# The output product of a gated MoE chunk in seven products of eight on token halves, for 12 of 24 chunks

## Chip, cores and metric

The kernel runs on one core of one Trainium2 chip. The metric is the device time of one execution in microseconds (us); lower is better. Three executions of the kernel before took 2841.73 to 2842.45 us, median 2842.4 us.

## What is computed

The reference takes a real tensor of 4 x 3072 x 256, transforms it by a Fourier transform along both axes, and passes the real part through two gated layers. The change lies at the end of the first layer:

```python
h = np.maximum(x @ w_in, 0.0)
u, v = (h[..., :d_ff // 2], h[..., d_ff // 2:])       # d_ff // 2 = 512
v_n = (v - mu) / np.sqrt(var + 1e-06)
v_s = np.einsum('ts,bsd->btd', w_spatial, v_n) + b_spatial[None, :, None]
gated = u * v_s
return (gated @ w_out).astype(np.float32)              # w_out: 512 x 256
```

The product `gated @ w_out` is what the kernel calls the second product: for each of 4 batches and 3072 tokens, 512 inner values and 256 outputs.

## The kernel before

All products run on TensorE in the type fp32r, each number being split in a high and a low part; a product is three matmuls (`mm3`, lines 259 to 263): high by high, high by low, low by high. ScalarE makes the high part (a cast), VectorE the low part (a subtraction).

**Stages.** Up to about 254 us the Fourier transform and the first layer's input product run, and U and V go to DRAM. From there to about 1752 us the spatial product `w_spatial @ v_n` runs, as two passes (p = 0, 1) over a pair of batches, each in seven block products instead of eight (`ORDER` = 3, 5, 1, 7, 4, 2, 6) of three token chunks of 512 columns (c = 0, 1, 2): 42 "leaves". After that the second layer runs to the end.

**A leaf** has six steps (`kp`). In each step TensorE does 24 matmuls of 512 columns: two k by four blocks d of 128 gate rows by three of `mm3`, into four PSUM banks. The banks of one leaf are `base` to `base + 3`, and the next leaf has the other four. While a leaf runs, VectorE works off the four banks of the leaf before (`evacuate`, step 0 to 3, one bank each). In the four products 5, 4, 2, 6 (`FINAL`) this yields the finished gate of a chunk: one operation makes `g` from the bank and the sums kept, mostly another one keeps a sum for later, line 1240 multiplies by `max(U, 0)`, ScalarE casts the high part (1246), VectorE makes the low part (1248). So there are 24 chunks with a second product, each done in the leaf behind its own.

**The second product before** (`second`, line 1276): at the end of step 4 for the output half o = 0, at the end of step 5 for o = 1. Each is four blocks d by `mm3` = 12 matmuls of 512 columns, into a bank that is already worked off; ScalarE copies the result (1287), and its queue sends both halves to DRAM (1289).

**Order on the queues.** Each engine works in order. In each step VectorE has first the `evacuate` of the leaf before, then the operands of three steps ahead (`advance`, `LEAD` = 3): where the block product needs it, a sum of two blocks of the spatial weights (933), and the low part (950); at the last chunk of a product also V blocks (929, 950). These take their ring slots as TensorE gives them back. SyncE's queue (SP) issues the loads in the order of the program; a load into a buffer in use waits there, and what is behind it waits too.

**U tiles** (`load_u`, 1257): four tiles of 128 x 512 for each chunk, in two buffers. U of d = 0 and 1 is loaded in step 4 of the chunk's own leaf; U of d + 2 is issued when line 1240 of d has been put into the program, and waits for that instruction.

**The last leaf** runs d by d from its third step on, its second product falls between the first groups of the second layer, and preparations for that layer (`split_wg`, `split_wv`, `x_steps`) run on VectorE and ScalarE meanwhile.

Of the kernel before, what the change touches and what calls it, by code (L numbers as in the profile page):

```python
# [10 lines left out]
F32 = mybir.dt.float32  # L11
# [12 lines left out]
DM = 256  # L24
# [136 lines left out]
def layouts(x, moe_w_in, moe_w_spatial, moe_b_spatial, moe_w_out, moe2_w_gate, moe2_w_val, moe2_w_out):  # L161
# [18 lines left out]
    for at in (0, 32, 64):  # L180
# [5 lines left out]
    wt = w.reshape(6, 512, 24, P).transpose(0, 3, 2, 1)  # L186
    wg, wv = (w.reshape(2, P, 12, P) for w in (moe2_w_gate, moe2_w_val))
    arrays = {
        "xh": xh,
# [4 lines left out]
        "bt": moe_b_spatial[tau].reshape(1, S),  # L194
        "w_out": moe_w_out.reshape(4, P, DM).transpose(1, 0, 2).reshape(P, 2, 512),

# [43 lines left out]
def tile_kernel(ctx: ExitStack, tc: tile.TileContext, t: dict, out: bass.AP):  # L240
# [926 lines left out]

    wo = [gp.tile([P, 2, 512], F32R, tag=f"wo{n}", name=f"wo{n}") for n in "hl"]
# [3 lines left out]
    taken, begun, stores = [], [], []  # L1172

    def background():

        new = lambda: gp.tile([P, 512], F32, tag="cv", name="cv", bufs=4)
        if taken:
            words, kind, i = taken.pop()
            begun.append((from64_first([words], new), kind, i))
        elif begun:  # L1180
            first, kind, i = begun.pop()
            value, = from64_rest(first, new())
            if kind == "second":
                split(wo[0][:, i, :], wo[1][:, i, :], value)
            elif kind == "out":
                stores.append((wv_d[i // 2][:, i % 2 * 512 : i % 2 * 512 + 512], value))
            else:

                a11, a12, a22, a21 = (value[:, k * P : k * P + P] for k in range(4))
                sums = new()  # L1190
                s1, s2, s3, s4 = (sums[:, k * P : k * P + P] for k in range(4))
                for s, x, y, op in (
                    (s1, a21, a22, ALU.add),
                    (s2, s1, a11, ALU.subtract),
                    (s3, a11, a21, ALU.subtract),
                    (s4, a12, s2, ALU.subtract),
                ):
                    nc.gpsimd.tensor_tensor(out=s, in0=x, in1=y, op=op)
                stores.append((wg_d[i][:, 0:384], value[:, 0:384]))
                stores.append((wg_d[i][:, 384:896], sums))  # L1200
        else:
            for to, value in stores:
                nc.sync.dma_start(to, value)
            stores.clear()
            if todo64:
                src, kind, i = todo64.pop(0)
                words = st_tile([P, 1024], U32, "words")
                load64(words, src)
                taken.append((words, kind, i))

    def evacuate(leaf, ps, d, side):
# [26 lines left out]
        if g is None:  # L1238
            return
        nc.vector.scalar_tensor_tensor(out=g, in0=side["u"][d], scalar=0.0, in1=g, op0=ALU.max, op1=ALU.mult)  # L1240
        if "parts" in side:
            gh, gl = (x[at] for x in side["parts"])
        else:
            gh = gp.tile([P, 512], F32R, tag="gh", name="gh", bufs=4)
            gl = gp.tile([P, 512], F32R, tag="gl", name="gl", bufs=4)
        nc.scalar.copy(gh, g)
        finish_gate(side)
        side["low"] = lambda: nc.vector.tensor_tensor(out=gl, in0=g, in1=f(gh), op=ALU.subtract)
        side["g"].append((gh, gl))
        if d < 2:  # L1250
            load_u(side, d + 2)

    def finish_gate(side):
        if "low" in side:
            side.pop("low")()

    def load_u(side, d):
        u = gp.tile([P, 512], F32, tag="u", name="u", bufs=2)
        nc.sync.dma_start(u, side["u_of"][:, d, :])
        side["u"].append(u)  # L1260

    def side_loads(leaf, side):
        p, i, c = leaf
        if i in (3, 4, 5):
            at = ((3 if i == 3 else 0) + c) * 512
            side["bias"] = gp.tile([P, 512], F32, tag="bias", name="bias")
            nc.sync.dma_start(side["bias"], t["bt"][:, at : at + 512].to_broadcast([P, 512]))
        if i in FINAL:
            mem, th = FINAL[i]
            at = (3 * th + c) * 512  # L1270
            side["u"] = []
            side["u_of"] = u_d[2 * p + mem][:, :, at : at + 512]
            for d in range(2):
                load_u(side, d)

    def second(leaf, o, bank, side):

        p, i, c = leaf
        mem, th = FINAL[i]
        finish_gate(side)  # L1280
        ps = banks(bank)
        for d in range(4):
            at = (d % 2) * 256 + o * P
            mm3(ps, [w[:, d // 2, at : at + P] for w in wo], side["g"][d], d == 0, d == 3)
        if o == 0:
            side["x2"] = gp.tile([P, 2, 512], F32, tag="x2", name="x2", bufs=1)
        nc.scalar.copy(side["x2"][:, o, :], ps)
        if o == 1:
            nc.scalar.dma_start(x2_d[(2 * p + mem) * 6 + 3 * th + c], side["x2"])

# [67 lines left out]
    def load_raw(j):  # L1358
        raw = []
        for c, n in zip(pairs[j], "hl"):  # L1360
            r = gp.tile([P, 2, 512], F32, tag=f"wo{n}", name="raw")
            nc.sync.dma_start(r, x2_d[c])
            raw += [r[:, 0, :], r[:, 1, :]]
        return raw
# [14 lines left out]
    for n, leaf in enumerate(leaves[:-1]):  # L1379
        p, i, c = leaf  # L1380
        base = 4 * (n % 2)
        ps = [banks(base + d) for d in range(4)]
        side = {"g": []}
        for kp in range(6):
            if before is not None:
                if kp < 4:
                    evacuate(before[0], before[1][kp], kp, before[2])
                else:
                    finish_gate(before[2])
            advance(6 * n + kp + LEAD, 2)  # L1390
# [4 lines left out]
            for k in range(2):  # L1395
                for d in range(4):
# [19 lines left out]
    ps = [banks(base + d) for d in range(4)]  # L1416
    side = {"g": []}
    raw = cp.tile([P, 4, 512], F32, tag="c12", name="raw0")
# [3 lines left out]
    for kp in range(2):  # L1422
# [8 lines left out]
        evacuate(before[0], before[1][kp], kp, before[2])  # L1431
    side_loads(leaf, side)
    advance(6 * n + 5, 0)
    finish_job()
    for d in (2, 3):
        evacuate(before[0], before[1][d], d, before[2])
    finish_gate(before[2])
    wv0 = [cp.tile([P, 8, DM], F32R, tag=f"c1{k}", name=f"wv{k}") for k in range(2)]
# [4 lines left out]
    for d in range(4):  # L1443
        for kp in range(2, 6):
            product(ps, leaf, kp, d)
        if d == 0:
            split_wg(0, staged_b[0])
            split_wv(0, staged_b[1])
        if d < 3:
            evacuate(leaf, ps[d], d, side)  # L1450
        if d == 1:
            second(before[0], 0, 4 - base + 2, before[2])
            split_wg(1, staged_b[2])
# [6 lines left out]
        if d == 2:  # L1460
            second(before[0], 1, 4 - base + 3, before[2])
            for step in steps[2:6]:
                step()
    before = (leaf, ps, side)
    wst = A["w"].tile([P, 1024], F32, tag="wl", name="wst")
# [34 lines left out]
    def gates(n):  # L1500
        g = G[n]
        nc.vector.tensor_tensor(out=g["s2"], in0=g["s2"], in1=g["t7"], op=ALU.mult)
        g["g"] = [[gp.tile([P, 512], F32R, tag="g" + x, name="g" + x, bufs=4) for x in "hl"] for _ in range(2)]

    def p67(n, prev):
        g = G.get(n)
        if g:
            g["t2"] = gp.tile([P, 512], F32, tag="cv", name="t2", bufs=4)
            g["t7"] = gp.tile([P, 512], F32, tag="u", name="t7", bufs=2)
            part(g["a"], n, "s2", "t2")  # L1510
            nc.scalar.copy(g["t2"], g["a"])  # L1511
# [15 lines left out]
    def outputs(n, k, os=(0, 1)):  # L1527
# [6 lines left out]
        if fb == 11:  # L1534
            c = pairs[j][k]
            at = slice(c * 512, c * 512 + 512)
            last = j + 1 == len(pairs)
            ot = gp.tile([P, 2, 512], F32, tag="wo" + "hl"[k] if last else "x2", name="ot", bufs=1)
            for o in range(2):
                if last and k == o == 1:  # L1540
                    pieces = (ot[:, o, :256], gp.tile([P, 2, 512], F32, tag="x2", name="ot", bufs=1)[:, 0, :256])
                    for h, (queue, piece) in enumerate(zip((nc.sync, nc.scalar), pieces)):
# [9 lines left out]
    for n in range(len(groups) + 2):  # L1552
# [24 lines left out]
        if n == 0:  # L1577
            steps[7]()
            second(leaf, 0, base, side)
            second(leaf, 1, base + 1, side)  # L1580
            for k in range(2):
# [8 lines left out]
        if j == 0:  # L1590
# [4 lines left out]
            if fb == 3:  # L1595
                x = cp.tile([P, 8, DM], F32R, tag="c12", name="wv2")
                wvs.append([x[:, 0:4, :], x[:, 4:8, :]])
                wst2 = gp.tile([P, 1024], F32, tag="x2", name="wst2", bufs=1)
                nc.sync.dma_start(wst2, wv_d[2])
# [32 lines left out]
```

## Time and profile before

| | |
|---|---|
| median of three executions | 2842.4 us (2841.73 to 2842.45) |
| profiled execution, its own time | 2841.18 us |
| span of the profiled execution | 2839.1 us |
| TensorE busy, matmul | 2827.8 us, 100% of the span, 12630 instructions |
| TensorE busy, weight load | 2360.2 us, 83% |
| VectorE busy | 1998.9 us, 70% |
| ScalarE busy | 1416.4 us, 50% |
| granted clock of TensorE | 1.000 over the whole span (the level of 2.4 GHz) |

The span runs from the first to the last instruction; 2.1 us of the execution's time lie around it. A matmul's entry lasts from its start to its modelled end and overlaps the next one: a group's mean is no measure of how often one can start. What one matmul costs is the distance from its start to the next start. The entries of VectorE overlap in the same way by a little.

### The profile page before, as it was taken

How to read it: one execution, taken by the hardware profiler on the slowest of the kernel's cores; microseconds unless marked ns; L12 is line 12 of the kernel's file. 1: busy time of each engine (PE TensorE's matmuls, PEld its weight loads, DVE VectorE, ACT ScalarE, POOL GpSimd, SP SyncE). 2: the span in 40 equal slices, each digit the busy share in tenths (PEclk: the TensorE clock that was granted, in tenths of full speed). 3: DMA queues.
4: the chain of work that ended last, by engine and by line, in shares of the span. 5: the costliest groups of instructions: out<-in, count | busy, mean ns of one | idle time of the engine just before them, and what ended most of it. 6: DMA issues, size and time to landing. Idle time of an engine off the chain costs nothing.

```text
span 2839.1 us, 34286 instructions
## 1 busy us (share of the span) xinstructions
PE 2827.8 (100%) x12630; PEld 2360.2 (83%) x12630; DVE 1998.9 (70%) x2936; ACT 1416.4 (50%) x2264; POOL 235.5 (8%) x348
## 2 busy tenths in 40 slices
PE   9999999999999999999999999999999999999999
PEld 7998888888888888888888888888888888888887
DVE  8877757778847666677756666876667666766665
ACT  6886434334424424433424424665655565656565
POOL 5984000011000000000000000000000000000000
PEclk9999999999999999999999999999999999999999
DMA  8888757778847766677866683100000000000000
GB/s 300 292 314 324 274 198 260 266 261 299 275 143 261 257 227 238 213 268 262 284 207 213 214 285 108 61 23 30 30 30 1 30 30 30 23 8 30 30 15 15
DMA packets 150953, 470.89 MB, mean 166 GB/s; under 512 B 16769, under 2 KB 18689, under 8 KB 150401
## 3 DMA queue, kind: packets, MB, share of 16 engines
q1 hardware_dynamic: 144448, 440.52, 45.0%
q0 software_dynamic: 2448, 14.82, 1.4%
q10 hardware_dynamic: 3888, 13.37, 1.2%
q8 instruction: 98, 1.61, 0.2%
q14 instruction: 71, 0.57, 0.1%
HBM read 386.07 MB, written 82.58 MB: 165 GB/s over the span
## 4 chain that ended last, share of the span: by engine, by line
PE 96%; DVE 2%; DMA 1%; ACT 1%; issue 0%; SPq 0%; ACTq 0%; DVEq 0%
PE bank L261 30%; PE bank L262 30%; PE bank L263 30%; PE psv L262 1%; PE psv L263 1%; PE psv L261 1%; PE psu L261 1%; PE psu L262 1%; PE psu L263 1%; PE psf L261 1%; PE psf L262 1%; PE psf L263 1%; DMA st<-v_d 1%; PE psv L730 0%; PE psu L768 0%
## 5 line engine op out<-in xcount | busy, mean ns | idle before, releaser
L262 PE MATMUL bank<-wl,vh 128*128 128x512 f32 x2016 | 784.4, 389 | 0.2 <-DVE wl L950 0.2
L261 PE MATMUL bank<-wh,vh 128*128 128x512 f32 x2016 | 784.3, 389 | 0.0
L263 PE MATMUL bank<-wh,vl 128*128 128x512 f32 x2016 | 784.2, 389 | 0.0
L942 ACT CAST wh<-st 128x1024 fp32r<-128x1024 f32 x249 | 260.9, 1049 | 382.9 <-PE bank L263 231.0
L262 PEld LDWEIGHTS bank<-wl,vh 128*128 128x128 f32 x2016 | 378.4, 188 | 79.5 <-DVE wl L950 0.8
L261 PEld LDWEIGHTS bank<-wh,vh 128*128 128x128 f32 x2016 | 378.4, 188 | 78.5
L263 PEld LDWEIGHTS bank<-wh,vl 128*128 128x128 f32 x2016 | 378.4, 188 | 78.3
L950 DVE TENSOR_TENSOR wl<-st,wh 128x1024 fp32r<-128x1024 f32 x249 | 306.8, 1233 | 169.4 <-ACT wh L942 168.9
L261 PE MATMUL bank<-x,wgh 128*128 128x512 f32 x673 | 262.4, 390 | 0.5 <-ACT t L1511 0.4
L1497 DVE TENSOR_TENSOR t<-t,bank 128x512 f32<-128x512 f32 x144 | 98.9, 687 | 231.4 <-PE bank L263 231.4
L262 PE MATMUL bank<-x,wgh 128*128 128x512 f32 x673 | 261.8, 389 | 0.0
L263 PE MATMUL bank<-x,wgl 128*128 128x512 f32 x673 | 261.8, 389 | 0.0
L933 DVE TENSOR_TENSOR st<-st 128x1024 f32<-128x1024 f32 x177 | 217.7, 1230 | 50.5 <-DMA st<-in_wt 50.5
L1520 DVE TENSOR_TENSOR gl<-s,gh 128x512 fp32r<-128x512 f32 x288 | 199.4, 692 | 57.8 <-ACT gh L1518 44.4
L262 PE MATMUL bank<-gl,wv 128*128 128x512 f32 x576 | 224.1, 389 | 0.0
L261 PE MATMUL bank<-gh,wv 128*128 128x512 f32 x576 | 224.1, 389 | 0.0
L263 PE MATMUL bank<-gh,wv 128*128 128x512 f32 x576 | 224.1, 389 | 0.0
L916 ACT ACTIVATE st<-st,ln_all 128x512 f32<-128x512 f32 x162 | 123.3, 809 | 140.5 <-DMA st<-v_d 115.7
L1485 ACT ACTIVATE s<-s 128x512 f32<-128x512 f32 x144 | 91.0, 632 | 153.8 <-DVE s L1484 153.7
L261 PEld LDWEIGHTS bank<-x,wgh 128*128 128x128 f32 x673 | 126.3, 188 | 28.5 <-ACT s L1482 0.9
L263 PEld LDWEIGHTS bank<-x,wgl 128*128 128x128 f32 x673 | 126.3, 188 | 26.3
L262 PEld LDWEIGHTS bank<-x,wgh 128*128 128x128 f32 x673 | 126.3, 188 | 26.0
(267 smaller groups left out, 4490.4 us busy)
## 6 DMA issues: line engine op xcount, KB each, us to landing
st<-in_wt SPq DMA_DIRECT2D x424, 512.0 KB, 5.5
st<-v_d SPq DMA_DIRECT2D x140, 512.0 KB, 4.7
u_d<-tu SPq DMA_DIRECT2D x64, 384.0 KB, 5.4
u<-u_d SPq DMA_DIRECT2D x96, 256.0 KB, 5.7
v_d<-tv SPq DMA_DIRECT2D x92, 256.0 KB, 5.1
x_d<-x ACTq DMA_DIRECT2D x24, 512.0 KB, 4.9
raw<-x_d SPq DMA_DIRECT2D x24, 512.0 KB, 7.1
xt<-in_xh SPq DMA_DIRECT2D x23, 512.0 KB, 5.2
```

Of the source, the lines that this page charges most:

```text
L261: nc.tensor.matmul(out=ps, lhsT=w[0], rhs=x[0], start=first, stop=False, **kw)
L262: nc.tensor.matmul(out=ps, lhsT=w[0], rhs=x[1], start=False, stop=False, **kw)
L263: nc.tensor.matmul(out=ps, lhsT=w[1], rhs=x[0], start=False, stop=last, **kw)
L916: nc.scalar.activation(st[:, k, :], st[:, k, :], AF.Identity, scale=scale[:, at], bias=shift[:, at])
L933: nc.vector.tensor_tensor(out=tiles[0], in0=tiles[0], in1=tiles[1], op=op)
L942: nc.scalar.copy(hl[0], st)
L950: eng.tensor_tensor(out=hl[1], in0=st, in1=f(hl[0]), op=ALU.subtract)
L1485: nc.scalar.activation(s1, s1, AF.Sigmoid)
L1497: nc.vector.tensor_tensor(out=g["t2"], in0=g["t2"], in1=g["b"], op=ALU.add)
L1520: nc.vector.tensor_tensor(out=l, in0=s, in1=f(h), op=ALU.subtract)
```

## The change

For 12 of the 24 chunks (`SEVEN`: in both passes the chunks of product 5 with c = 0, of 4 with c = 2, of 2 with c = 0 and 1, of 6 with c = 0; in pass 0 also those of 6 with c = 1 and 2) the second product is done in seven products instead of eight. The 2 x 2 blocks are: output half by gate block within a pair of gate blocks (d = 0, 1 and d = 2, 3), and token halves of 256 columns (`HC`). VectorE makes four differences of gate halves for each pair; the sums of blocks of `w_out` are made once on GpSimd, and `wo` doubles in width. TensorE does 7 x 2 x 3 = 42 matmuls of 256 columns for the chunk. They stand at the end of step 2 (six of the products of pair 0), 3 (the seventh) and 4 (all seven of pair 1). Step 5 has `combine`: one copy on ScalarE and six sums on VectorE put the two outputs together from four banks.

The other 12 chunks keep 24 matmuls of 512 columns (`plain`), now as 12 at the end of step 3, 6 at step 4, 6 at step 5. There is one U buffer instead of two: U of d + 1 is issued behind line 1240 of d. Each chunk's output goes out in two DMAs of 256 KB instead of one of 512 KB. Stores that were put off go out at step 0 of a leaf behind a `FINAL` one (`send_stores`). In the last leaf the U loads come behind the last `evacuate` of the leaf before, and one split comes between two of these. The tiles concerned move from the pool `gp` to a pool `mp`, which is closed and opened anew ahead of the second layer.

```diff
@@ background @@
-                split(wo[0][:, i, :], wo[1][:, i, :], value)
...
+                if kind == "second":
+                    for at, src in ((slice(0, 512), value), (slice(512, 1024), sums)):
+                        split(wo[0][:, i, at], wo[1][:, i, at], src)
@@ evacuate @@
         nc.vector.scalar_tensor_tensor(out=g, in0=side["u"][d], scalar=0.0, in1=g, op0=ALU.max, op1=ALU.mult)
+        if d < 3:
+            load_u(side, d + 1)
+        finish_gate(side)
+        if leaf not in SEVEN:
+            if "parts" in side or d < 3:
+                take_piece(side, "g", d, g)
+            else:
+                side["late"] = lambda: take_piece(side, "g", d, g)
+            return
+        if d % 2 == 0:
+            side["raw"] = g
+            if d == 0:
+                take_piece(side, 0, 0, g[:, 0:HC])
+            return
+        b1, b2 = side.pop("raw"), g
+        if d == 1:
+            take_piece(side, 0, 1, b2)
+        else:
+            take_piece(side, 1, 0, b1[:, 0:HC])
+            side["late"] = lambda: take_piece(side, 1, 1, b2)
+        ta, tb = (gp.tile([P, 512], F32, tag="cv", name="t", bufs=4) for _ in range(2))
+        for to, x, y in (
+            (ta[:, 0:HC], b1[:, HC:], b1[:, 0:HC]),
+            (tb[:, 0:HC], b2[:, HC:], b1[:, HC:]),
+            (ta[:, HC:], b2[:, HC:], ta[:, 0:HC]),
+            (tb[:, HC:], b2[:, 0:HC], ta[:, HC:]),
+        ):
+            tt(out=to, in0=x, in1=y, op=ALU.subtract)
+        take_piece(side, d // 2, 2, ta)
+        take_piece(side, d // 2, 3, tb)
...
-        if d < 2:
-            load_u(side, d + 2)
...
     def load_u(side, d):
-        u = gp.tile([P, 512], F32, tag="u", name="u", bufs=2)
+        u = mp.tile([P, 512], F32, tag="u", name="u", bufs=1)
...
+    def second(side, pair, terms, bank):
+        for term in terms:
+            w, piece, half, acc, at = TERMS[term]
+            first = acc not in side["acc"]
+            if first:
+                side["acc"][acc] = banks(bank + acc)
+            w = slice(WO_AT[w] * P, WO_AT[w] * P + P)
+            mm3(
+                side["acc"][acc][:, at * HC : at * HC + HC],
+                [x[:, pair, w] for x in wo],
+                [x[:, half * HC : half * HC + HC] for x in side["g"][pair, piece]],
+                first,
+                pair == 1,
+                skip_group_check=True,
+            )
...
+    def combine(side, part, both, to):
+        x, y, z, w = (side["acc"][k] for k in range(4))
+        tt = nc.vector.tensor_tensor
+        p1, u2 = part[:, 0:HC], part[:, HC:]
+        nc.scalar.copy(p1, x[:, 0:HC])
+        tt(out=u2, in0=p1, in1=x[:, HC:], op=ALU.add)
...
@@ the loop over the leaves @@
-            if before is not None:
-                if kp < 4:
-                    evacuate(before[0], before[1][kp], kp, before[2])
-                else:
-                    finish_gate(before[2])
+            if kp == 0 and final:
+                send_stores()
+            if before is not None and kp < 4:
+                evacuate(before[0], before[1][kp], kp, before[2])
+            if final and kp == 4:
+                before[2].pop("late")()
+                finish_gate(before[2])
+            if seven and kp == 5:
+                combine_cv(before[2])
             advance(6 * n + kp + LEAD, 2)
...
-            if before is not None:
-                if kp >= 4 and before[0][1] in FINAL:
-                    second(before[0], kp - 4, 4 - base + kp - 2, before[2])
+            if final and not seven and kp == 3:
+                for o in range(2):
+                    plain(before[2], 0, o, 4 - base + 2 + o)
+            if final and not seven and kp > 3:
+                plain(before[2], 1, kp - 4, None)
+                plain_out(before[2], kp - 4)
+            if seven and kp in (2, 3, 4):
+                second(before[2], kp // 4, ((1, 6, 5, 7, 4, 3), (2,), (1, 6, 5, 7, 4, 3, 2))[kp - 2], 4 - base)
+            if final and kp == 5:
+                send(before[0], before[2])
```

## Rows read from the trace of the kernel before

**Rows 1.** The page, busy time of each engine: us (share of the span) x instructions.

```profile
span 2839.1 us, 34286 instructions
PE 2827.8 (100%) x12630; PEld 2360.2 (83%) x12630; DVE 1998.9 (70%) x2936; ACT 1416.4 (50%) x2264; POOL 235.5 (8%) x348
```

**Rows 2.** The page, chain that ended last: shares of the span by engine.

```profile
PE 96%; DVE 2%; DMA 1%; ACT 1%; issue 0%; SPq 0%; ACTq 0%; DVEq 0%
```

**Rows 3.** Timeline, TensorE, spatial product: start us, duration us, engine, line, operation.

```profile
299.72 0.39 PE L261 MATMUL bank<-wh,vh 128*128 128x512 f32 x1
...
309.92 0.39 PE L261 MATMUL bank<-wh,vh 128*128 128x512 f32 x1
```

**Rows 4.** Timeline, TensorE, around 121 us: the narrowest fp32r matmuls, 384 columns.

```profile
121.39 0.33 PE L261 MATMUL psu<-ph,gh 128*128 128x384 f32 x1
...
125.03 0.39 PE L261 MATMUL psv<-gh,ph 128*128 128x512 f32 x1
```

**Rows 5.** Timeline, TensorE and its weight loads (PEld), a restart after a wait.

```profile
40.80 0.19 PEld L261 LDWEIGHTS psv<-gh,ph 128*128 128x128 f32 x1 [0.36 <-ACT ph L453]
40.81 0.50 PE L261 MATMUL psv<-gh,ph 128*128 128x512 f32 x1
40.91 0.19 PEld L262 LDWEIGHTS psv<-gl,ph 128*128 128x128 f32 x1
```

**Rows 6.** Groups by line and shape: second product, one of its three lines; xcount | busy us, mean ns.

```profile
L261 PE MATMUL bank<-gh,woh 128*128 128x512 f32 x184 | 71.6, 389 | 0.0
...
L261 PE MATMUL bank<-tail,woh 128*128 128x512 f32 x8 | 3.1, 390 | 0.0
```

**Rows 7.** Timeline, VectorE, back to back, at the gate of product 5, c = 0.

```profile
384.08 0.69 DVE L1240 SCALAR_TENSOR_TENSOR g<-u,g 128x512 f32<-128x512 f32 x1
384.68 1.22 DVE L950 TENSOR_TENSOR wl<-st,wh 128x1024 fp32r<-128x1024 f32 x1
385.81 0.68 DVE L1223 TENSOR_TENSOR g<-c,bank 128x512 f32<-128x512 f32 x1
```

**Rows 8.** Windows, leaves (0,2,1), (0,2,2): us, busy (x) of PE, PEld, DVE, ACT, POOL.

```profile
809.00:847.10 38.10, 38.10 (x169) 31.53 (x168) 16.94 (x23) 10.89 (x14) 0.00 (x0) 1.00 0.53 176
847.10:885.20 38.10, 38.10 (x170) 31.53 (x169) 30.67 (x37) 22.50 (x28) 0.00 (x0) 1.00 0.77 263
```

**Rows 9.** Timeline, TensorE, leaf (0,2,2): its first matmul and the first of the second product.

```profile
847.12 0.39 PE L261 MATMUL bank<-wh,vh 128*128 128x512 f32 x1
...
874.32 0.39 PE L261 MATMUL bank<-gh,woh 128*128 128x512 f32 x1
```

**Rows 10.** Timeline, VectorE, the same leaf: one step's operands, gate steps, last low part, a wait.

```profile
853.45 1.22 DVE L950 TENSOR_TENSOR vl<-st,vh 128x1024 fp32r<-128x1024 f32 x1
...
857.12 0.68 DVE L1234 TENSOR_TENSOR g<-c,bank 128x512 f32<-128x512 f32 x1
...
865.60 1.22 DVE L933 TENSOR_TENSOR st<-st 128x1024 f32<-128x1024 f32 x1
...
870.33 0.69 DVE L1248 TENSOR_TENSOR gl<-g,gh 128x512 fp32r<-128x512 f32 x1
...
875.94 1.46 DVE L929 SCALAR_TENSOR_TENSOR st<-st,ln_all 128x512 f32<-128x512 f32 x2 [1.75 <-ACT st L916]
```

**Rows 11.** U loads: all 96, us to landing; DMA view of 430 to 435 us; of 763 to 764.5 us.

```profile
DMA to landing us min/median/max: 2.6/5.7/8.2
...
u<-u_d SPq DMA_DIRECT2D x1, 256.0 KB, 4.2
...
u<-u_d SPq DMA_DIRECT2D x2, 256.0 KB, 8.1
```

**Rows 12.** Waits of TensorE: line, waited for: us in total, times, longest us.

```profile
PE bank L261 <- ACT t L1511: 0.4, 1, 0.4
...
PE bank L262 <- DVE wl L950: 0.2, 1, 0.2
```

**Rows 13.** Groups by line and shape: the sums of weight blocks on GpSimd.

```profile
L1198 POOL TENSOR_TENSOR cv<-cv 128x128 f32<-128x128 f32 x48 | 38.9, 831 | 764.7 <-DVE cv L304 763.7
```

More of the change, by code (lines that the diff above doesn't have):

```diff
@@ L1172, in tile_kernel, with send_stores @@
     taken, begun, stores = [], [], []
+    def send_stores():
+        for to, value in stores:
+            nc.sync.dma_start(to, value)
+        stores.clear()
     def background():
@@ L1241, in evacuate, with take_piece @@
+        take_piece(side, d // 2, 2, ta)
+        take_piece(side, d // 2, 3, tb)
+    HC = 256
+    def take_piece(side, pair, i, src):
+        n = src.shape[-1]
         if "parts" in side:
-            gh, gl = (x[at] for x in side["parts"])
+            hi, lo = (x[:, i, :] for x in side["parts"])
         else:
[L1244 to L1247, printed above, removed]
@@ L1248, in evacuate @@
[L1248 to L1251 removed]
+            k = (2, 1, 3, 2)[i] if pair == "g" else i
+            hi, lo = (mp.tile([P, n], F32R, tag=f"{x}{k}", name=f"b{x}") for x in "hl")
+        nc.scalar.copy(hi, src)
+        side["g"][pair, i] = (hi, lo)
+        side["lows"].append(lambda: nc.vector.tensor_tensor(out=lo, in0=src, in1=f(hi), op=ALU.subtract))
@@ L1272, in side_loads @@
             side["u_of"] = u_d[2 * p + mem][:, :, at : at + 512]
-            for d in range(2):
-                load_u(side, d)
-    def second(leaf, o, bank, side):
+            load_u(side, 0)
+    TERMS = {
+        1: ("a11", 0, 0, 0, 0),
+        6: ("s2", 2, 1, 0, 1),
+        5: ("s1", 2, 0, 1, 0),
+        7: ("s3", 3, 0, 1, 1),
+        3: ("s4", 1, 1, 2, 0),
+        4: ("a22", 3, 1, 2, 1),
+        2: ("a12", 1, 0, 3, 0),
+    }
+    SEVEN = {(p, i, c) for p in range(2) for i, c in ((5, 0), (4, 2), (2, 0), (2, 1), (6, 0))}
@@ new lines, in tile_kernel, with plain, plain_out @@
+    SEVEN |= {(0, 6, 1), (0, 6, 2)}
+    WO_AT = {"a11": 0, "a12": 1, "a22": 2, "a21": 3, "s1": 4, "s2": 5, "s3": 6, "s4": 7}
+    def plain(side, pair, o, bank):
+        if pair == 0:
+            side["acc"][o] = banks(bank)
+        for d in (2 * pair, 2 * pair + 1):
+            at = WO_AT[f"a{o + 1}{d % 2 + 1}"] * P
+            mm3(side["acc"][o], [x[:, pair, at : at + P] for x in wo], side["g"]["g", d], d == 0, d == 3)
+    def plain_out(side, o, to=None):
+        to = gp.tile([P, 512], F32, tag="cv", name="y", bufs=4) if to is None else to
+        nc.scalar.copy(to, side["acc"][o])
+        side.setdefault("to", []).append(to)
@@ L1278, in second, with combine_cv, send @@
+    def combine_cv(side):
+        combine(side, *(lambda a: (a[0], a[1], a[2:]))([gp.tile([P, 512], F32, tag="cv", name="y", bufs=4) for _ in range(4)]))
+    def send(leaf, side):
         p, i, c = leaf
         mem, th = FINAL[i]
[L1280 to L1286, printed above, removed]
@@ L1446, in tile_kernel @@
         if d == 0:
-            split_wg(0, staged_b[0])
+            for o in range(2):
+                plain(before[2], 0, o, 4 - base + 2 + o)
+            before[2].pop("late")()
+            finish_gate(before[2])
             split_wv(0, staged_b[1])
@@ L1451, in tile_kernel @@
         if d == 1:
-            second(before[0], 0, 4 - base + 2, before[2])
+            plain(before[2], 1, 0, None)
+            plain_out(before[2], 0)
             split_wg(1, staged_b[2])
@@ L1460, in tile_kernel @@
         if d == 2:
-            second(before[0], 1, 4 - base + 3, before[2])
+            plain(before[2], 1, 1, None)
+            plain_out(before[2], 1)
+            send(before[0], before[2])
             for step in steps[2:6]:
                 step()
-    before = (leaf, ps, side)
     wst = A["w"].tile([P, 1024], F32, tag="wl", name="wst")
@@ L1578, in tile_kernel @@
             steps[7]()
-            second(leaf, 0, base, side)
-            second(leaf, 1, base + 1, side)
+            for o in range(2):
+                for pair in range(2):
+                    plain(side, pair, o, base + o)
+            mix.close()
+            mp = pool(ra, "mp", 1, "right")
+            last_x2 = mp.tile([P, 2, 512], F32, tag="x2", name="x2", bufs=1)
+            for o in range(2):
+                plain_out(side, o, last_x2[:, o, :])
+            send(leaf, side)
             for k in range(2):
```

67 lines of the change are left out of this document (41 added, 26 removed).

## The prediction, made before the changed kernel ran

> **What bounds the kernel now.** I read the page from the top: busy time first, then the chain that ended last, then the waits, and last the timeline of the stage that the change touches. TensorE is busy for 2827.8 of 2839.1 us, VectorE for 70% of the span [rows 1]; 96% of the chain is TensorE [rows 2]; the waits of TensorE that the view lists behind the spatial product's start are 0.2 and 0.4 us [rows 12]. So TensorE sets the time nearly everywhere, and work taken from it shortens the run one for one, as long as no other engine falls behind it. Busy time does not tell what a matmul costs, since an entry of 0.39 us overlaps the next. The distance of starts does: from 299.72 to 309.92 us there are 45 starts of 512 columns, so 10.20 / 45 = 226.7 ns each [rows 3]. In leaf (0,2,2) 120 matmuls go before the second product, 874.32 - 847.12 = 27.2 us, again 226.7 ns [rows 3, 9]: no gap at all.
>
> **What TensorE saves.** The second product is 192 x 3 = 576 matmuls in 24 chunks, 24 for each [rows 6], or 24 x 226.7 ns = 5.44 us a chunk. After the change 12 chunks take 42 matmuls of 256 columns, a shape that the trace does not have in fp32r. The nearest is 384 columns: 21 starts from 121.39 to 125.03 us, 3.64 / 21 = 173.3 ns [rows 4]. The two prices lie on a line: 128 columns more cost 53.4 ns, which is 128 columns at 2.4 GHz, and 13.3 ns remain as a fixed part of each matmul (173.3 - 160.0 and 226.7 - 213.3). So at 256 columns I take 106.7 + 13.3 = 120.0 ns. A chunk in the seven form then costs 42 x 120.0 = 5.04 us, 0.40 us less than 5.44, and not an eighth (0.68) less, since the fixed part is paid 42 times instead of 24. Twelve chunks give 4.8 us. The point from which it gains nothing is 5440 / 42 = 129.5 ns a matmul, so only 9.5 ns above my price.
>
> Can the weight load hold that pace? Its entry is 188 ns long, more than 120; but at 384 columns loads follow each other at 173 ns, so an entry is not its cost [rows 4]. After a wait, two loads start at 40.80 and 40.91 us, 0.11 us apart, and the matmul between them has 0.50 us instead of 0.39, 0.11 of them spent on its own load [rows 5]. So a load occupies its path for about 0.11 us, and hides behind a matmul of 120 ns, with 10 ns to spare. Bounds: no faster than the loads follow each other, 107 to 110 ns, and no slower than the narrowest matmul seen, 173 ns. I take 120, the line through two measured widths, which the loads' row allows.
>
> That row speaks for overlap of a load with the matmul ahead of it: a load starts at 40.91, where the first matmul really begins. The Trainium skill, "TensorE: Matmul & The Clock Gate", section "The mechanism" of Part 3, says that loads overlap matmuls in flight only when they go to another row group. All loads here go to the full array, and 226.7 ns for 213.3 ns of columns leave no room for 0.11 us of load in series: this case's rows disagree with that sentence. By it a matmul of 256 columns would cost about 107 + 120 = 227 ns and the change would lose 12 x (42 x 0.227 - 5.44) = 49 us; I give that no chance.
>
> **What VectorE and ScalarE pay.** VectorE's entries overlap too; by starts, 512 columns cost 0.60 us and 1024 cost 1.13 us [rows 7], so 256 cost about 0.33 us. For a seven chunk: before, 4 low parts x 0.60 = 2.40 us. After: low parts 2 x (0.33 + 3 x 0.60) = 4.26, differences 8 x 0.33 = 2.64, combine 0.33 + 0.60 + 4 x 0.33 = 2.25, together 9.15, so 6.8 us more in a leaf of 37.7 us. In leaf (0,2,1) VectorE is busy for 16.94 of 38.10 us, and 24 us are well within the leaf. In leaf (0,2,2), which does chunk (2,1) and also makes V blocks, it is 30.67 [rows 8], and 30.7 + 6.8 = 37.5 fills it. Operands are made three steps (16.3 us) ahead, so being full for one leaf does not stop TensorE by itself; the gate pieces have an earlier time at which they are needed, and that decides.
>
> I follow VectorE through leaf (0,2,2), from the leaf's first matmul as zero. The chunk ahead is of the seven kind too, so nothing of it stands behind step 5, and bank 0 is complete nine matmuls (2.0 us) before zero; combine and one low part take VectorE to about -1.7. Gate d = 0: three operations, 0.1. Operands of step 0: 857.12 - 853.45 = 3.67 us [rows 10], 3.8. Gate d = 1, 5.6; one narrow low part and four differences (1.65), 7.2. Operands, 10.9. Gate d = 2, 12.7; three low parts, 14.5. TensorE wants them at the end of step 2, 72 x 226.7 ns = 16.3: 1.8 us to spare. Pair 1: operands 18.2, gate d = 3 20.0, differences 21.3, operands of step 3 4.73 us [rows 10] 26.0, low parts 2.13, 28.2; wanted at 27.2 + 21 x 0.12 = 29.7: 1.5 us to spare. Before, the last low part ended near 871 for a use at 874.32 [rows 9, 10]. The cover is thin: one wait of 1.75 us, as VectorE has it for the V blocks at 875.94 [rows 10], uses it up. I book 0.25 us for each of the two such leaves, 0.5 in all (bounds 0 and 3.4 each, below).
>
> ScalarE casts 4 more pieces and copies less, about 1 us more on an engine busy for 22.50 of 38.10 us there [rows 8]; nothing.
>
> **One U buffer.** SP waited for line 1240 of d before too, so nothing new is held back there at d = 0 and 1; at d = 2 one more wait stands before the loads of that step. New is that line 1240 of d + 1 now waits for a load issued only after d. With a landing time L, pair 0 is ready at 0.1 + 2 (L + 0.60) + 1.8 = 3.1 + 2L, wanted at 16.3: it holds up to L = 6.6 us. The landings are 2.6 / 5.7 / 8.2 us; a load sent alone took 4.2, two sent together took 8.1 [rows 11], and after the change each goes alone. I take 4.2 to 5.7, so 11.5 to 14.5 and no wait of TensorE; behind line 1240 on VectorE stand the operands of the same step, with their lead of three steps. For the 12 plain chunks the first use is at the end of step 3, later still.
>
> **The rest.** The sums of `w_out` on GpSimd: 2 x 4 x 0.83 us [rows 13], for which ScalarE's cast and VectorE's low part wait up to 3.3 us, twice, in the second leaf; operands are three steps ahead, so nothing, and 6.6 us if that cover were gone. One DMA more a chunk on ScalarE's queue, behind its own work: nothing. Put-off stores at step 0 hold SP for GpSimd at most 3.3 us, while loads run two steps ahead of the operands: nothing. In the last leaf the four U loads follow one another, and gate d = 1 and the parts behind it come later; I book 0.5 us, about the waits there now (0.4 for one line, [rows 12]); bounds -0.6, when the waits of [rows 12] go, and 2.0, one late landing of 5.7 against 3.7.
>
> **Sum.** For the profiled execution: 2841.2 - 4.8 + 0.5 + 0.5 = 2837.4 us. The median lies 1.2 us above that execution: 2838.6 us.
>
> **Rivals.**
> 1. *VectorE late.* In both leaves with chunk (2,1) it meets waits of 1.75 us in each of steps 0 to 2, as it does later in that leaf [rows 10]: 5.25 - 1.8 = 3.4 us late, twice, 6.9 us in place of the 0.5 booked for these leaves. 2842.4 - 4.8 + 6.9 + 0.5 = 2845.0. For it: 37.5 of 37.7 us full. Against it: up to 870.33 that leaf shows no wait. Chance 0.20, most of it between 2840 and 2845.
> 2. *The U chain decides, slower.* Place: line 1240 of d = 1 and 2 in the 12 seven chunks. At L = 8.1 us pair 0 comes at 19.3, 3.0 us late; 12 x 3.0 - 4.8 = +31, 2874 us. It gives back the whole gain from L = 6.8 on (0.4 us late a chunk). For it: the longest landings. Against it: these came from loads sent in pairs. Chance 0.08.
> 3. *The narrow matmul does not scale.* At 173 ns, 42 x 173.3 = 7.28 us, 1.84 more than 5.44; 12 x 1.84 = 22 us, 2864.5. It loses from 129.5 ns on. Against it: the straight line of two widths. Chance 0.06.
> 4. *The fixed part goes, only the loads pace.* At 107 ns, 42 x 107 = 4.49 us; 12 x 0.95 = 11.4 us, 2831.0. Against it: 13.3 ns at both widths. Chance 0.06. The same page of the Trainium skill ("Back-to-back issue gap") gives columns at 2.4 GHz + 2.5 ns; by that estimate 512 columns would cost 215.8 ns and the seven form would save 12 x (24 x 215.8 - 42 x 109.2) = 7.1 us, but here the row for 512 columns shows 226.7.
>
> **How the numbers follow.** Forecast 2838.6, chance 0.60, with a range of its own from 2836.3 (the waits of [rows 12] gone, 2837.0, less the 0.7 us by which executions differ) to 2841. The range of 8 in 10 leaves out rivals 2, 3 and 4 (0.20) and takes in rival 1: 2836.3 to 2845.0. A measurement of this kernel can tell about 0.2%, 5.7 us, from no change. Faster than 2836.7: rival 4 and an edge of the forecast, 0.10. Slower than 2848.1: rivals 2 and 3, 0.14. Within: 0.76.
>
> **What would show it.** Starts of the 256-column matmuls 120 ns apart, 504 of them, and 288 fewer of 512; a leaf with a seven chunk 37.7 us long instead of 38.1. No wait of TensorE for low parts of pieces or for `combine`; VectorE near full in leaf (0,2,2). U loads landing in 3 to 6 us. Wrong if the starts are over 129.5 ns apart, if TensorE waits at the ends of steps 2 and 4, or if the second layer's start is later than the leaves' gain explains.

## The result: slower by 17 us

| | median, us (lowest to highest) | span of the profiled execution | ratio to before |
|---|---|---|---|
| before | 2842.4 (2841.24 to 2842.45) | 2839.1 | 1 |
| after | 2859.73 (2857.06 to 2862.18) | 2857.7 | 1.0062, 95% interval 1.0049 to 1.0075 |

The forecast was 2838.6 us with a range to 2845.0: the time lies 15 us outside it, on the other side. The profiled execution of after took 2859.51 us. The page of after, busy time and the chain that ended last, against [rows 1, 2]:

```profile
PE 2830.4 (99%) x12846; PEld 2369.0 (83%) x12846; DVE 2088.2 (73%) x3154; ACT 1429.9 (50%) x2302; POOL 240.6 (8%) x356
...
PE 87%; DMA 5%; DVE 5%; ACT 2%; issue 1%; SPq 0%; POOL 0%; ACTq 0%; DVEq 0%; POOLq 0%
```

TensorE was 96% of the chain and is 87% now; DMA stands at 5% for 1% before, VectorE at 5% for 2%. VectorE is busy for 89 us more (2088.2 against 1998.9), which fits the price of 6.8 us for each of twelve chunks (82). The waits of TensorE in after (line, waited for, us in total, times, longest), against [rows 12], with the first loads left out:

```profile
PE bank L262 <- DVE c L1240: 6.9, 2, 4.7
...
PE bank L262 <- ACT y L1342: 3.6, 1, 3.6
...
PE bank L262 <- DVE g L1245: 1.5, 1, 1.5
PE bank L263 <- DVE wl L951: 1.2, 1, 1.2
```

None of them is for the low part of a gate; `combine` (lines 1368 and 1375) has 1.0 us in two waits, both at the start of leaf (0,6,0). Line 1240 of after is the second operation of `evacuate` for product 4, which reads the bank.

**The matmul of 256 columns** costs what was booked. Timeline of TensorE in after, against [rows 3, 4]:

```profile
794.76 0.28 PE L263 MATMUL bank<-bl,woh 128*128 128x256 f32 x1
794.88 0.28 PE L264 MATMUL bank<-bh,wol 128*128 128x256 f32 x1
...
796.68 0.28 PE L264 MATMUL bank<-bh,wol 128*128 128x256 f32 x1
796.80 0.40 PE L262 MATMUL bank<-wh,vh 128*128 128x512 f32 x1
797.04 0.40 PE L263 MATMUL bank<-wl,vh 128*128 128x512 f32 x1
```

From 794.76 to 796.80 us there are 17 starts: 120.0 ns each. Eleven of the twelve leaves with a seven chunk take 37.74 us for 38.08, 0.34 us less (0.40 was booked; the first starts of 512 columns behind them are 0.24 us apart instead of 0.227).

**Where the time went.** I take each leaf's length from its first matmul to the next leaf's first. In us, after less before: start of the spatial stage +0.8; the eleven leaves -3.7; leaf (0,4,2) +6.55, (1,1,0) +6.45, (1,4,2) +2.59, (1,7,0) +1.07, (0,6,0) +0.80, (0,2,2) +0.62, (0,5,0) +0.37; the last leaf +1.78; the second layer +1.3. That is 18.6, the difference of the spans. The two large ones and a quiet one in the view of windows (columns as in [rows 8]):

```profile
733.70:778.30 44.60, 39.94 (x169) 32.59 (x168) 34.43 (x42) 22.53 (x28) 0.00 (x0) 0.96 0.74 253
778.30:816.10 37.80, 37.80 (x188) 32.08 (x187) 24.55 (x42) 11.22 (x16) 0.00 (x0) 1.00 0.41 140
...
1218.30:1262.90 44.60, 41.04 (x170) 33.40 (x170) 29.48 (x35) 13.16 (x16) 0.00 (x0) 0.92 0.72 249
```

Leaf (0,4,2) works off chunk (0,4,1), which is a *plain* chunk, and makes V blocks. VectorE there, in after: line 1248 multiplies by U.

```profile
731.83 0.68 DVE L1248 SCALAR_TENSOR_TENSOR g<-u,g 128x512 f32<-128x512 f32 x1
...
743.23 0.69 DVE L1248 SCALAR_TENSOR_TENSOR g<-u,g 128x512 f32<-128x512 f32 x1 [4.19 <-DMA u<-u_d]
...
754.24 0.69 DVE L1248 SCALAR_TENSOR_TENSOR g<-u,g 128x512 f32<-128x512 f32 x1 [3.67 <-DMA u<-u_d]
...
760.90 0.69 DVE L1240 TENSOR_TENSOR c<-bias,bank 128x512 f32<-128x512 f32 x1
```

And SP's queue in the same leaf (a row's duration is the time that the queue spent on it, waiting included):

```profile
735.24 2.84 SPq L883 DMA_DIRECT2D st<-v_d  x2
738.17 0.38 SPq L1302 DMA_DIRECT2D u<-u_d  x1
738.60 8.56 SPq L883 DMA_DIRECT2D st<-in_wt  x2
747.21 0.90 SPq L883 DMA_DIRECT2D st<-v_d  x2
748.15 0.42 SPq L1302 DMA_DIRECT2D u<-u_d  x1
...
749.67 8.49 SPq L883 DMA_DIRECT2D st<-v_d  x2
758.26 0.38 SPq L1302 DMA_DIRECT2D u<-u_d  x1
```

U of d = 0 is used up at 732.5, yet U of d = 1 is sent at 738.17, 5.7 us later: the ring loads of the step stand ahead of it on SP. VectorE waits for it until 743.23. The work that frees the next ring slot stands behind that gate on VectorE:

```profile
745.58 1.22 DVE L951 TENSOR_TENSOR vl<-st,vh 128x1024 fp32r<-128x1024 f32 x1
```

The second of the two ring loads at 738.60 goes out at 746.82, when this line has ended; so SP sits there for 8.56 us, and U of d = 2 stands behind it. Two turns of this circle, 5.7 + 4.2 us of standing behind ring loads beside landings of 5.1 and 6.1 us, put the gate of d = 2 at 754.24. Behind that gate come 5.3 us of other work on VectorE, mostly the step's operands, and the bank of d = 3 is read at 760.90 for a product that was ready to use it at 756.8. A third turn, 3.3 us, falls behind that read. TensorE's restart in after:

```profile
756.60 0.39 PE L264 MATMUL bank<-bh,wol 128*128 128x512 f32 x1
761.65 0.50 PE L262 MATMUL bank<-bh,woh 128*128 128x512 f32 x1 [4.66 <-DVE c L1240]
761.98 0.56 PE L263 MATMUL bank<-bl,woh 128*128 128x512 f32 x1
762.35 0.63 PE L264 MATMUL bank<-bh,wol 128*128 128x512 f32 x1
762.77 0.63 PE L262 MATMUL bank<-bh,woh 128*128 128x512 f32 x1
```

At its pace TensorE would have gone on at 756.83, so the wait costs 4.8 us. The rest of the 6.55 is the clock: starts are 0.43 us apart for 3.4 us, at a granted clock of 0.51 from 762 to 765 us (the level of 1.2 GHz), the third column from the end:

```profile
762.00:765.00 3.00, 3.00 (x9) 2.32 (x8) 2.53 (x4) 2.30 (x3) 0.00 (x0) 0.51 1.00 404
```

In before the same leaf has the same hold-up, only covered. Its gate of d = 0 and SP's queue, before:

```profile
729.64 0.68 DVE L1240 SCALAR_TENSOR_TENSOR g<-u,g 128x512 f32<-128x512 f32 x1
...
733.01 4.24 SPq L882 DMA_DIRECT2D st<-v_d  x2
737.34 0.38 SPq L1259 DMA_DIRECT2D u<-u_d  x1
```

U of d = 2 was sent 7.0 us after its buffer came free, but U of d = 1 lay in the other buffer. These rows could be read before the change ran.

### The profile page after: what moved, and what is told of

The parts are those of the page before. It is cut to its first block, busy times and chain, and to the rows that moved or that the text cites. A ratio compares the mean times of both kernels' runs of the same rounds, so it can differ in the third digit from the quotient of the medians.

```text
span 2857.7 us, 35095 instructions
## 1 busy us (share of the span) xinstructions
PE 2830.4 (99%) x12846; PEld 2369.0 (83%) x12846; DVE 2088.2 (73%) x3154; ACT 1429.9 (50%) x2302; POOL 240.6 (8%) x356
## 4 chain that ended last, share of the span: by engine, by line
PE 87%; DMA 5%; DVE 5%; ACT 2%; issue 1%; SPq 0%; POOL 0%; ACTq 0%; DVEq 0%; POOLq 0%
PE bank L262 26%; PE bank L263 26%; PE bank L264 26%; DMA st<-v_d 2%; DMA u<-u_d 1%; DVE wl L951 1%; PE psv L263 1%; PE psv L264 1%; PE psv L262 1%; PE psu L262 1%; PE psu L263 1%; PE psu L264 1%; DMA xs<-in_xs 1%; DVE st L934 1%; PE psf L262 1%
## 5 line engine op out<-in xcount | busy, mean ns | idle before, releaser
L1289 ACT CAST bh<-g 128x256 fp32r<-128x256 f32 (+1 forms) x92 | 51.9, 565 | 227.5 <-DVE g L1248 131.3
L262 PEld LDWEIGHTS bank<-x,wgh 128*128 128x128 f32 x673 | 126.3, 188 | 30.0 <-DVE s L1601 1.5
```

The source lines that it names most:

```text
L262: nc.tensor.matmul(out=ps, lhsT=w[0], rhs=x[0], start=first, stop=False, **kw)
L1289: nc.scalar.copy(hi, src)
```

## Experiments

The first theory, H: one buffer puts U's issue in series with the ring loads ahead of it on SP, and that circle makes the loss. The rivals: the early use of the banks by the plain order; VectorE filled by the seven form; U's landing as such. Each kernel is timed against before on the same chip. The leaves are read from one profiled execution of each kernel, which lies up to 4.3 us off its median.

| kernel | median, us (lowest to highest) | ratio, 95% interval | leaves (0,4,2) / (1,1,0) / (1,4,2), us |
|---|---|---|---|
| b_u1 | 2860.14 (2859.86 to 2863.44) | 1.0065, 1.005 to 1.008 | 46.29 / 39.78 / 44.64 |
| a_plain | 2860.45 (2857.45 to 2861.85) | 1.0062, 1.0047 to 1.0077 | 44.69 / 39.69 / 40.91 |
| a_plain_2u | 2845.31 (2843.98 to 2849.69) | 1.0012, 1.0003 to 1.0022 | 38.16 / 38.08 / 38.08 |
| a_pool | 2844.83 (2843.97 to 2846.0) | 1.0007, 0.9997 to 1.0017 | 38.08 / 38.08 / 38.08 |
| a_pool_tail | 2844.46 (2842.54 to 2847.35) | 1.0008, 0.9999 to 1.0017 | 38.08 / 38.46 / 38.08 |
| a_plain_pool | 2849.21 (2844.95 to 2853.86) | 1.0023, 1.0013 to 1.0033 | 38.41 / 38.76 / 38.08 |
| b_u1_pool | 2846.79 (2844.1 to 2849.53) | 1.0016, 1.0007 to 1.0025 | 38.08 / 39.74 / 38.08 |
| a_act | 2846.29 (2843.91 to 2850.21) | 1.0015, 1.0006 to 1.0024 | 38.45 / 38.43 / 38.13 |
| a_own45 | 2848.15 (2845.36 to 2851.98) | 1.0019, 1.001 to 1.0027 | 38.08 / 38.08 / 38.08 |
| a_two26 | 2841.06 (2839.43 to 2844.72) | 0.9995, 0.9986 to 1.0004 | 38.08 / 38.61 / 38.08 |

Before stood at 2842.48 us beside the first four, 2842.26 beside the next four and 2842.71 beside the last two. In before the three leaves take 38.08.

**b_u1: one U buffer in the kernel before**, with the last leaf's U loads behind the last `evacuate` and the second layer's tile `t7` in two tiles of one buffer each, as one U buffer needs it.

```diff
-        u = gp.tile([P, 512], F32, tag="u", name="u", bufs=2)
+        u = gp.tile([P, 512], F32, tag="u", name="u", bufs=1)
...
-        if d < 2:
-            load_u(side, d + 2)
+        if d < 3:
+            load_u(side, d + 1)
```

> The kernel before with one U buffer and nothing else of the change: U of d + 1 is issued behind line 1240 of d, and in the last leaf the U loads come behind the last gate of the leaf before, as they must then. Theory 'queue' (with one buffer the load of U is issued late, behind ring loads on SP's queue that wait for VectorE, which itself waits for U): 4 to 20 us slower than before, with VectorE waiting for U as in the changed kernel (38 us there, 0.5 before) in leaves that also make V blocks. Theory 'vector' (the stalls come from the 6.8 us of work that a chunk in seven products adds to VectorE): within 2 us of before.

2860.14 us, as much as the whole change costs, without a product in seven and without the plain order. That the two totals agree so nearly is luck: leaf (1,4,2) loses 6.56 us here and 2.59 in after, leaf (1,1,0) 1.70 and 6.45. SP's queue in leaf (0,4,2) of b_u1 shows the circle again:

```profile
735.05 4.24 SPq L882 DMA_DIRECT2D st<-v_d  x2
739.37 0.38 SPq L1259 DMA_DIRECT2D u<-u_d  x1
739.81 9.13 SPq L882 DMA_DIRECT2D st<-in_wt  x2
```

**a_plain: the changed kernel with no chunk in seven products**, and **a_plain_2u: the same with two U buffers**, loaded two ahead as before.

```diff
-    SEVEN = {(p, i, c) for p in range(2) for i, c in ((5, 0), (4, 2), (2, 0), (2, 1), (6, 0))}
-    SEVEN |= {(0, 6, 1), (0, 6, 2)}
+    SEVEN = set()
```

> The changed kernel with no chunk in seven products: all 24 in the plain form, one U buffer. Theory 'queue': the stalls stay and the 4.8 us of TensorE are lost, 2857 to 2867 us. Theory 'vector': the stalls go with the extra work, 2841 to 2845 us.

> As the changed kernel with no chunk in seven products, and two U buffers loaded as before (U of d = 0 and 1 in step 4 of the chunk's own leaf, U of d + 2 behind d). It differs from a_plain in the U buffers alone, and from before in the place of the second product (steps 3 to 5 instead of 4 and 5). Theory 'queue': 2841 to 2845 us, as before. A rival, 'early use' (the plain form's first products at the end of step 3 come before VectorE has worked off the bank they write, whatever the U loads do): as a_plain, 2855 us or more.

Without the seven form nothing gets better (2860.45). With the second buffer back, VectorE's wait for U (us in total, times) falls from the first of these rows, a_plain, to the second, a_plain_2u:

```profile
  DMA u<-u_d: 40.8, 38
```

```profile
  DMA u<-u_d: 0.4, 1
```

The three leaves are undisturbed, although the plain order still uses the bank of d = 3 at the end of step 3. So the early use costs next to nothing by itself; it is the place where a late U is felt in after (line 1240), as the low parts were in b_u1. The time is 0.3 us over the range given. What a_plain_2u keeps over before is the last leaf (38.57 for 38.08 us), the second layer (1089.7 for 1088.4) and 1.0 us in leaves (0,5,0) and (1,7,0).

**a_pool: the changed kernel with U loaded on GpSimd's queue.** One buffer, as in after.

```diff
-        nc.sync.dma_start(u, side["u_of"][:, d, :])
+        nc.gpsimd.dma_start(u, side["u_of"][:, d, :])
```

> The changed kernel with its U loads issued on GpSimd's queue instead of SP's, still one buffer. Theory 'queue': the stalls of 4.8, 3.7, 2.4 and 1.6 us go, VectorE's wait for U falls from 38 us to under 15, and the time is 2837 to 2843 us, up to 5 us below before. Theory 'vector': no change, 2857 to 2862 us. A third theory, 'landing' (U's landing time alone is too long for one buffer, whichever queue issues it): 2855 us or more.

14.9 us come back, and the three large stalls are gone; the time is 1.8 us over the range given. But VectorE's wait for U was expected under 15 us and is longer than in after. Who waited for U in after, in a_pool, and the landings of a_pool (us in total, times; us to landing):

```profile
  DMA u<-u_d: 38.1, 29
```

```profile
  DMA u<-u_d: 45.6, 26
...
DMA to landing us min/median/max: 2.9/3.7/6.8
```

So neither the landing (median 3.7 us in both) nor VectorE's wait for U, summed over the run, makes the loss: in chunk (0,4,1) U of d = 1 to 3 takes 3.0, 5.6 and 5.0 us to land in a_pool, and VectorE waits for none of them. The same leaf in a_pool, timeline of SP, GpSimd and VectorE:

```profile
741.59 5.23 SPq L883 DMA_DIRECT2D st<-in_wt  x2
...
743.40 0.55 POOL L1302 DMA_DIRECT2D u<-u_d  x1 [6.58 <-DVE g L1248]
...
752.14 0.68 DVE L1248 SCALAR_TENSOR_TENSOR g<-u,g 128x512 f32<-128x512 f32 x1
```

U of d = 2 goes out 0.3 us after line 1248 of d = 1 has ended (0.3 us over all 72 of d = 1 to 3), not 3.3 to 5.7 us as in the two chunks (p,4,1) of after, and is there when VectorE comes to it. SP is held for 5.23 us, not 8.56.

**b_u1_pool and a_act: the same test in the kernel before, and on ScalarE's queue.** The edit is that of a_pool, on b_u1, and with `nc.scalar` on after.

> The kernel before with one U buffer (2860.1 us with U on SP's queue), U's loads on GpSimd's queue. Theory H, U stands on SP behind ring loads that wait for slots which VectorE frees only after its U: off that queue 2842 to 2846 us, leaves (0,4,2) and (1,4,2) near 38.1 for 46.3 and 44.6. Rival B, one buffer alone makes VectorE late, whatever queue loads it: 2856 us or more.

> The changed kernel with its U loads on ScalarE's queue. Theory H: any queue without the ring loads will do, but here U stands behind ScalarE's casts and its wait for VectorE holds casts up, so 2843 to 2850 us, leaf (0,4,2) under 40. Rival: only GpSimd's queue is free enough; the wait in ScalarE's queue moves the stall to the casts, 2855 us or more.

Both came out as H has it: 2860.14 becomes 2846.79 and 2859.73 becomes 2846.29. With one buffer it is the queue of the ring loads that must not carry U, and GpSimd's is not special. (b_u1_pool lies 0.8 us above its range; leaf (1,1,0) still takes 39.74 us for 39.78, so its 1.7 us there are not U's queue. a_act has a loss of its own, 2.0 us in leaf (0,6,0), which was not followed up.)

**a_plain_pool: a_pool with no chunk in seven products.** The edit is that of a_plain.

> The changed kernel with U on GpSimd's queue and no chunk in seven products. Theory: the seven products are worth what the matmuls say, 12 leaves x 0.34 = 4.1 us, when no U stalls TensorE: 2844.8 + 4.1 = 2848.9 us, and no leaf but the last differs from 38.08 and 32.64 by over 1 us. Rival, VectorE's added work eats the gain: within 1 us of 2844.8.

2849.21 us; a_pool stands at 2844.83. By ratios, 1.0023 - 1.0007 = 0.0016 is 4.5 us, where 4.1 were expected. Each ratio is good to 0.0010, so by an estimate from the two intervals the difference is good to some 4 us and shows little more than its sign. The leaves are firmer: eleven of the twelve behind a seven chunk take 37.74 us in a_pool, all twelve 38.08 here. So the seven form is worth what its matmuls say once no U stalls TensorE. In after it showed nearly nothing (a_plain 2860.45, after 2859.73).

**a_own45: U on GpSimd's queue only for chunks (4,c) and (5,c).** Eight of the twelve seven chunks, those of products 2 and 6, are left on SP with one buffer; the expectation below counts ten, which is wrong.

```diff
+            side["own"] = i in (4, 5)
...
-        nc.sync.dma_start(u, side["u_of"][:, d, :])
+        (nc.gpsimd if side["own"] else nc.sync).dma_start(u, side["u_of"][:, d, :])
```

> The changed kernel with U's loads on GpSimd's queue only for chunks (4,c) and (5,c); chunks (2,c) and (6,c), ten of the twelve in seven products among them, keep one buffer on SP's queue. Theory H with its place: the stalls belong to leaves that make V's blocks, so the big ones (6.6, 6.5 and 2.6 us in leaves (0,4,2), (1,1,0), (1,4,2)) go, and what stays is the 1 us each of (0,2,2) and (0,6,0) and the tail: 2844.8 to 2847.5 us. Rival, U's turn-round stalls any chunk whose VectorE is full (the prediction's second rival, in the seven-product chunks): 2850 us or more.

The three large stalls are gone, so they come from chunks (4,c) and (5,c). That they come from plain ones, after says itself: the leaves behind the four seven chunks among these, (p,5,0) and (p,4,2), take 37.74 us there. Leaves (0,2,2) and (0,6,0) keep 38.48 and 38.84 us. There a seven chunk does lose: U of d = 3 of chunk (0,2,1) is sent 3.9 us after its buffer came free, in after too, and TensorE waits 0.9 us for `combine`. The time is 0.65 us over the range given. In the profiled execution the last leaf took 42.90 us: TensorE waited 0.8 us for a low part and 1.88 for VectorE to read a bank, which stood behind a gate whose U came 2.4 us late, and ran at a granted clock of 0.5 for 3.4 us after that:

```profile
1734.85 0.69 PE L262 MATMUL bank<-bh,woh 128*128 128x512 f32 x1 [1.88 <-DVE g L1245]
```

**a_pool_tail: a_pool with the last leaf's second products put back** behind the output blocks d = 1 and d = 2.

```diff
         if d == 0:
-            for o in range(2):
-                plain(before[2], 0, o, 4 - base + 2 + o)
...
         if d == 1:
-            plain(before[2], 1, 0, None)
+            for o in range(2):
+                plain(before[2], 0, o, 4 - base + 2 + o)
```

> The changed kernel with its U loads on GpSimd's queue (2844.8 us) and, besides, the last leaf's second products put back as before: both first halves after the leaf's second output block, both second halves after its third. Theory T, the moved products cost the tail 1.8 us (in the profile with U on GpSimd the last leaf took 38.57 for 38.08 and the second layer 1.3 to 2 us more, because its second output block ended 2.7 us later): 2843.0 us, last leaf 38.1, second layer 1088.4 to 1089. Rival, the tail is late because of U's landing, whatever the order: 2844.8 us again. The start of the spatial stage (258.0 us there, 254.1 to 255.9 in the other profiles) is taken for a matter of how the first loads land; if so it is 254 to 256 here, and the time up to 3 us less; if it is 258 again, U's queue costs there too.

Half a miss. The last leaf is back at 38.08 us, but the second layer takes 1092.6 us for 1090.5 in a_pool, and the time is the same. This profile is of the slowest execution (2847.35 us), and of the 2.1 us 1.3 are the clock: it was granted at 0.50 from 1757.2 to 1760.5, behind waits of 1.44 and 0.56 us (0.80 and 0.55 in a_pool, where it stayed at 1.00). VectorE in the last leaf of a_pool_tail:

```profile
1737.69 0.68 DVE L1245 TENSOR_TENSOR g<-c,bank 128x512 f32<-128x512 f32 x1
1741.22 0.69 DVE L1248 SCALAR_TENSOR_TENSOR g<-u,g 128x512 f32<-128x512 f32 x1 [2.84 <-DMA u<-u_d]
```

With the products put back, d = 1 comes earlier and waits 2.84 us for U, which the new order had hidden. So order and buffer were put back together in the next kernel. The start of the stage was 255.0 us here and 254.4 in a_plain_pool, so the 258.0 of a_pool is not U's queue. In a_pool and in b_u1_pool (257.9) the clock was at 0.5 for 3.4 us from 37 or 38 us on, in no other profile.

**a_two26: a second U buffer where one is free.** Chunks (2,c) and (6,c) keep no bias; its tile takes every other U there, loaded two ahead on SP as before. Chunks (4,c) and (5,c) are loaded on GpSimd's queue. The last leaf is as in a_pool_tail, with `side_loads` between the last two `evacuate`.

```diff
+        if side["two"] and d % 2:
+            u = gp.tile([P, 512], F32, tag="bias", name="u")
...
+            side["two"] = i in (2, 6)
```

> The changed kernel with a second U buffer for the chunks (2,c) and (6,c), which keep no bias and lend its tile: there U is loaded two ahead on SP's queue as before; chunks (4,c) and (5,c) have one buffer, loaded on GpSimd's queue. The last leaf's second products stand as before. Theory H+T (one buffer behind SP's ring loads cost the middle, one buffer and the new order the tail): 2842.3 - 4.1 for the seven products + about 1 for single waits in (0,5,0), (1,7,0) = 2839.2 us (2837.5 to 2841.5), last leaf 38.1, second layer within 0.5 us of the 1088.4 before. Rival, the tail is late for another reason of the change (the four last products, where tiles are closed and opened again): second layer again 1090 to 1092, 2841.5 to 2844 us.

2841.06 us, 1.65 us below before and 18.7 below after, the fastest kernel of this case; the interval of its ratio takes in 1, so it is not shown to beat before. The waits of TensorE in a_two26, first loads left out:

```profile
PE bank L262 <- ACT t L1635: 1.0, 1, 1.0
PE bank L263 <- DVE wl L951: 1.0, 1, 1.0
```

The last leaf is 38.08 us. The second layer is 1089.5 us, still 1.1 more than before, where 0.5 at most was expected and the rival said 1090 to 1092. Of it 0.6 is the wait for the copy `t` (1.0 us for the 0.4 of [rows 12]). That wait is 1.0 us in every run of the changed kernel, with one buffer or two, and 0.4 in before, b_u1 and b_u1_pool, so it goes with the changed second layer and not with U. Why the copy comes later there, and where the other half is, was not settled. Leaves (0,5,1), (1,1,0) and (1,7,0) together keep another 2.0 us.

## Why the prediction was wrong, step by step

- *What bounds the kernel, and the narrow matmul*: right. 120.0 ns at 256 columns, 504 times; 0.34 us a leaf for 0.40. Rivals 3 and 4 (173 and 107 ns) fall. The sentence of the Trainium skill that the prediction set aside ("TensorE: Matmul & The Clock Gate", "The mechanism" of Part 3) would have made it 227 ns; the rows from 794.76 us on say 120.0. An estimate by the formula in the same page of the Trainium skill, "Back-to-back issue gap", columns at 2.4 GHz + 2.5 ns, is 109.2 ns; these rows show more.
- *VectorE*: right in size. 0.25 us were booked for each of the leaves (0,2,2) and (1,2,2). In after the first takes 38.70 us, 1.0 more than the 37.74 of the others, and the leaf behind it 0.80 more than before; the second takes 37.74. But in a_pool, with the same work, leaf (0,2,2) takes 37.74 us, with VectorE busy for 35.55 of 37.70 us (37.5 forecast), and the leaf behind it 38.15: that lateness came of U too. Rival 1 falls.
- *One U buffer*: **this is the step that failed**, in the sentence "SP waited for line 1240 of d before too, so nothing new is held back there". Summed over the run that holds: SP stands at U's loads for 262 us in before and 243 in after. But it looked at what stands behind U on SP and not at what stands *ahead* of it. U was priced by its landing (4.2 to 5.7 us), and the landing is little different: median 3.7 us, and 5.1, 6.1 and 4.2 in chunk (0,4,1). The missing term is the time from the buffer's release to the issue: 5.7, 4.2 and 3.3 us in chunk (0,4,1), 5.6, 3.8 and 3.3 in (1,4,1). In before the same two chunks show 7.0 and 5.0, and 7.3 and 3.7, harmless with a second buffer. By the prediction's own formula with 7.0 + 4.2 for the first turn and 5.0 + 4.2 for the second, and 0.60 for each gate, pair 0 comes at 0.1 + 11.8 + 9.8 + 1.8 = 23.5, not 11.5 to 14.5.
- "*For the 12 plain chunks the first use is at the end of step 3, later still*": wrong in kind. The large stalls all come from chunks that the formula left out. At the end of step 3 not only the pieces of pair 0 are wanted but also the bank of d = 3, and VectorE reads that behind two turns of U *and* the operands of step 2: at 760.90, 27.2 us after the leaf's first matmul, where it was wanted 23.1 us after it.
- *Rival 2* (the U chain decides) had the right engine and sign, with chance 0.08, but the wrong place (the 12 seven chunks: in after only (0,2,1) loses, 1.0 us in its leaf and 0.8 in the next) and the wrong price (landing 8.1 us).
- *The last leaf*: 0.5 us booked, bounds -0.6 and 2.0; measured 1.78 in the leaf and 1.3 behind it. a_plain_2u and a_pool put 0.5 of the leaf's down to the new order. The rest comes with U on SP in after and a_own45 (42.90 us), but not in a_plain (38.54), so it is not settled. Of the 1.3, 0.6 is the wait for the copy `t`; the rest stays open, as does why the copy is late.
- *The sum*: -3.7 us of the -4.8 for the products came; against them stand 22.3 us of stalls, tail and start, where 1.0 was booked.

For leaf (1,1,0) the trace shows the releases (the copy of chunk (1,5,1)'s output, line 1342, behind ScalarE's wait of 6.31 us for V's ring load; U of d = 3 of that chunk had kept VectorE waiting for 2.7 us), and a_pool and a_own45 show that it goes when U leaves SP; the steps by which U delays that ring load were not tested one by one. It is not all U's: a_plain has U on SP and takes 39.69 us, and in b_u1_pool, where VectorE waits for no U of that chunk, ScalarE still waits 6.89 us for V's ring load and 1.7 us are lost.

## What to carry to other kernels

Before a buffer is given up, take the time from its release to the next issue on its queue for every load, not the median landing alone, and look at the worst stage: a hold-up that a second buffer hides becomes the period with one. With one buffer, a load that waits for a consumer does not belong on the queue that feeds the consumer's other work, since each then waits for the other. And cost a changed order at the first use of each bank, for the parts of the kernel that the change seems to leave alone as well.

## What the hardware showed beyond that

Behind TensorE's wait of 4.66 us the granted clock was 0.51 for about 3.4 us, and in leaf (1,1,0) 0.5 for 6.8 us, the first 1.3 of them still in the wait of 3.6 us: of the 13.0 us that these two leaves lost, 8.5 are the waits and 4.5 the slow matmuls behind them. The clock was not in the sum. The length of the wait alone did not decide it here: behind 2.26 us in leaf (1,4,2) the clock stayed at 1.00, behind 1.44 and 0.56 in a_pool_tail it fell to 0.50. One load issued by GpSimd took 0.55 us of that engine, on SP mostly 0.33 of the queue. Some kernels scattered more (a_act 2843.9 to 2850.2 us) than before did beside them (2841.11 to 2845.74), but a_pool, also with U off SP, did not (2843.97 to 2846.0), and a_plain_2u with U on SP did (to 2849.69); why was not looked into.
